# Attention and two MLPs on one core: high parts written in place, rows of maxima in one DMA, longer lags in the plan

## The chip, the cores and the metric

The kernel runs on one core of a Trainium2 chip. The metric is device microseconds of an execution; less is better.

## The reference

Queries are averaged in pairs of neighbours, so that 576 queries meet 1152 keys in each of 16 heads (2 batches of 8, head size 64). The heads are put side by side and go through two MLPs (512 to 2048 to 512), the first with a leaky ReLU, the second with SiLU. All is fp32.

```
q_pool = q.reshape(B, H, S // 2, 2, D).mean(axis=3)
scores = (1 / sqrt(D)) * q_pool @ k^T
attn = exp(scores - max(scores)); attn = attn / (sum(attn) + 1e-9)
x = (attn @ v), heads side by side: 1152 x 512
x = leaky_relu(x @ w_in, 0.01) @ w_out
h = x @ w2_in;  out = (h * sigmoid(h)) @ w2_out
```

## The kernel before

TensorE's fast fp32 form (FP32R) keeps too few bits, so operands are split into a high and a low part, which are multiplied apart and added in PSUM. Two heads j = 0, 1 make a pair p, of which there are eight; head j lies on partitions `own[j]` of what is loaded, the other half is `oth[j]`.

Preparing a pair (`prep`, from pair 1 on). K and Q of both heads are loaded (`knat`, `qnat`; one buffer each), GpSimd adds the two neighbouring queries (L481). ScalarE writes the high parts of both heads to `kf` and `qf` (L348), VectorE the low parts in place (L500, L505; for pair 1 GpSimd). DMAs on SP's queue then bring the parts to where TensorE wants them: `K2[p, j]` holds the high part of K on `own[j]` and the low part on `oth[j]`, `QH[p, j]` the high part of Q on both halves. `copy_ka` copies the high part of K once more to `KA`, whose other half is ones; `QL` holds the low part of Q and, on one row of its other half, minus the maxima of the scores. A score tile (`scores`, L661) is then two matmuls, K2 with QH and KA with QL, and already has the maximum taken off. Pair 0 (`prep_first`) is prepared in smaller pieces without these moves: ScalarE writes the high parts, and the second half of QH is a cast on VectorE for head 0 (L350).

Maxima come first and from high parts of Q alone: `max_tile` multiplies 128 queries by 384 keys (L574, L575, L578; 27 tiles a pair), VectorE reduces each tile to one column of `mx` (L582), `finish_max` reduces these to `mn` (L626), and `finish_rows` sends each column of 128 maxima as a row to QL by a DMA of its own. Pair 0 does it with whole rows of keys in three banks (L602, L607).

After the scores ScalarE takes the exps (L665), TensorE multiplies them with V (`pv`, L693), GpSimd adds them up over the key tiles (L682). `sums` adds over partitions (L721), and since the sums then lie in four rows, they go through DRAM and back (`d`, `cmp`) to be spread over 128 partitions for the reciprocal on VectorE (L756), through DRAM again (`d2`), and are broadcast to all partitions (`r`). `finish` multiplies the product with V by r on VectorE (L796), ScalarE writes its high part `xh` (L799), VectorE the low part `xl` (L800).

Six PSUM banks serve scores, maxima and sums in turn; two hold the product with V. A tile of maxima keeps its bank until VectorE has reduced it.

The order on every engine is made by `Plan`: a list of tasks with weights, lags, due times and tokens for buffers. Time in the plan goes forward, each engine takes the ready task with the earliest due time, and what is emitted then is that engine's order in the program. Due times are given in pairs of length `T` after `T0`: loads at `load`, the preparation at `prep`, maxima between the two values of `max`, the final product at `norm`. A wrong lag in the plan costs nothing by itself, but engines work in order, so that an instruction that is put too early holds what is behind it. The MLPs (L1058 on) have a plan of their own.

Of the kernel before, what the change touches and what calls it, by code (L numbers as in the profile page):

```python
# [18 lines left out]
def pooled_attention_two_mlps(  # L19
# [26 lines left out]
    t0=16.0,  # L46
    t=27.0,
    load=-1.7,
    prep=(-1.4, -1.35, -1.25, -1.15),
    prep1=(10.0, 11.0, 12.0, 13.0),  # L50
    max=(-0.97, -0.2),
    pv=4.0,
    sums=1.15,
    norm=1.55,
    dve_add=(),
    dve_last=tuple((t, j) for t in range(1, 9) for j in range(2)),
    k_pool=((1, 1), (0, 1)),
    lead=3,
    load0=8.0,
# [224 lines left out]
def attention(ctx, tc, q, k, v, xh, xl, weights, end_p):  # L284
# [141 lines left out]
    def prep_first(p, j, loads, out):  # L426
# [46 lines left out]
    def prep(p, loads, due, out):  # L473
# [34 lines left out]
        def move(src, dst, after, d):  # L508
            go = lambda: tuple(y.bitcast(F32) for y in (dst(), src()))
            return dma(d, go, after=after, lag=3.0)  # L510
# [5 lines left out]
        for i in range(n):  # L516
            take = () if i else ("kf",)
            kh.append(add("ACT", 0.21 + 0.84 / n, due[1], k_hi(i), after=[loads["k"][i], x], order=kh[-1:], take=take))
            kl.append(add(eng, 1.95 * w / n, due[1], k_lo(i), after=kh[-1:]))
        qh = add("ACT", 0.63, due[0], q_hi, after=[x])  # L520
        ql = add(eng, w, due[2], q_lo, after=[qh])
        users = {"kf": list(kl), "knat": [], "qnat": []}
        for j in range(2):
            d = due[2] + 0.2 * j
            a = move(lambda j=j: kf[p][own[j]], lambda j=j: K2[p, j][own[j]], kh, d)
# [4 lines left out]
            users["kf"].append(a)  # L530
            users["knat"] += bs
            cs = [move(lambda j=j: qf[p][own[j]], lambda j=j, r=r: QH[p, j][r], [qh], d) for r in own]
# [3 lines left out]
            for i in range(2):  # L536
                out["k", j, i] = [a] + bs
                out["kh", j, i] = [a]
# [7 lines left out]
    def copy_ka(p, j, out, due, after):  # L546
# [5 lines left out]
        else:  # L552
            go = lambda: (KA[p % 2, j][own[j]].bitcast(F32), K2[p, j][own[j]].bitcast(F32))
            out["ka", j, 0] = out["ka", j, 1] = [dma(due, go, after=out["kh", j, 0] + after, lag=3.0)]
# [3 lines left out]
    def max_tile(p, n, out, due):  # L558
# [9 lines left out]
        def pe():  # L568
# [61 lines left out]
    def finish_rows(p, j, units, t, out, due, after):  # L630
        for u in units:
            if u < NFULL:
                rows = [(j, slice(u * 128, (u + 1) * 128), slice(0, 128))]
            else:
                rows = [(i, slice(NFC, SQ), own[i]) for i in range(2)]
            for i, cs, ps in rows:
                go = lambda u=u, i=i, cs=cs, ps=ps: (
                    QL[p % 3, i][orow[i]:orow[i] + 1, cs].bitcast(F32), box["m", p, j][ps, u:u + 1].bitcast(F32)
                )
                out.setdefault(("mr", i), []).append(dma(due, go, after=[t] + after, lag=1.9))  # L640
# [46 lines left out]
    def pv(p, t, due, after, order):  # L687
        def go():
            for c in range(2):
# [8 lines left out]
        last = t == NKT - 1  # L698
        return add("PE", 1.27, due, go, after=after, order=order, take=() if t else ("v",), give=("vnat",) if last else ())
# [14 lines left out]
    def sums(p, after, due):  # L714
# [110 lines left out]
    for p in range(NP):  # L825
# [448 lines left out]
```

## Time and profile before

| | us |
|---|---|
| median of three runs | 681.51 (679.25 to 681.9) |
| profiled execution | 682.97 |
| its span, first to last instruction | 680.9 |
| PE busy | 648.1 |
| VectorE, GpSimd, ScalarE busy | 437.0, 392.3, 302.6 |
| granted TensorE clock, mean | 0.979 |

A busy PE overlaps its matmuls, so its busy time says where it idles and not how full it is. The granted clock is a share of full speed. The profile has three stages: a head until the first scores at 22.8 us, attention until 275.7 us, the MLPs until the end.

### The profile page before, as it was taken

Reading aid. Unit: us, or ns where it says so; the run is one execution under the profiler, and the core shown is the slowest. Engines: PE = TensorE matmul, PEld = TensorE weight load, DVE = VectorE, ACT = ScalarE, POOL = GpSimd, SP = SyncE. Lnnn points to the kernel's source line nnn. Section 1 sums busy time; section 2 is a strip of 40 time slices with the busy share of each in tenths; the row PEclk is TensorE's granted clock in tenths of the full one; section 3 lists DMA queues with packets and bytes.
Section 4 is the critical chain, followed back from the end, with each engine's and each line's share of the span. In section 5 each row is a group of like instructions: output and inputs, shape, how many; then the busy total and the mean of one; then the engine's idle time right before and its main releaser. Section 6 shows DMA issues by size and latency. Waiting matters only on the chain.

```text
span 680.9 us, 9990 instructions
## 1 busy us (share of the span) xinstructions
PE 648.1 (95%) x3616; PEld 523.2 (77%) x3616; DVE 437.0 (64%) x616; ACT 302.6 (44%) x629; POOL 392.3 (58%) x278
## 2 busy tenths in 40 slices
PE   3799999989798999999999999999999999999997
PEld 2566666656565666798998998989998898888986
DVE  7383748639484776686666676688989888522222
ACT  3345545546364555655443343355455553322120
POOL 8578979678696770575354354376666445432120
PEclk9899999979797999999999999999999999999999
DMA  8685556758584711032223223222223322000012
GB/s 208 134 232 158 121 160 139 205 129 240 134 226 93 164 49 50 6 120 92 94 93 94 93 92 94 94 93 84 80 86 123 124 94 93 0 1 1 0 47 93
DMA packets 36248, 72.08 MB, mean 106 GB/s; under 512 B 15820, under 2 KB 15848, under 8 KB 36200
## 3 DMA queue, kind: packets, MB, share of 16 engines
q1 hardware_dynamic: 36200, 71.46, 37.7%
q8 instruction: 28, 0.46, 0.3%
q14 instruction: 20, 0.16, 0.1%
HBM read 49.81 MB, written 2.42 MB: 77 GB/s over the span
## 4 chain that ended last, share of the span: by engine, by line
PE 80%; DMA 9%; DVE 7%; SPq 2%; issue 1%; ACT 1%; POOL 0%; DVEq 0%; POOLq 0%; ACTq 0%
PE ph L1058 30%; PE po L1129 15%; PE pf L1178 14%; PE psum L661 8%; PE psum L693 7%; DMA r<-d 3%; DVE mx L582 3%; PE psum L578 3%; SPq L343 2%; DMA ql<-mn 2%; DMA d<-sum 2%; PE psum L602 1%; DVE pvs L796 1%; DMA qnat<-in_q_dram 1%; DVE mn L607 1%
## 5 line engine op out<-in xcount | busy, mean ns | idle before, releaser
L1111 POOL TENSOR_TENSOR gl<-a,gh 128x512 fp32r<-128x512 f32 (+1 forms) x64 | 97.2, 1519 | 142.7 <-ACT gh L1105 76.1
L682 POOL TENSOR_TENSOR acc<-acc,e 128x576 f32<-128x576 f32 x98 | 147.5, 1533 | 24.0 <-ACT e L665 23.7
L665 ACT ACTIVATE e<-psum 128x288 f32<-128x288 f32 x288 | 102.5, 411 | 97.1 <-PE psum L661 81.7
L582 DVE TENSOR_REDUCE mx<-psum 128x1 f32<-128x384 f32 x189 | 93.9, 547 | 59.4 <-PE psum L578 56.2
L1058 PE MATMUL ph<-xh,w0h 128*128 128x320 f32 (+1 forms) x384 | 109.0, 338 | 0.5 <-ACT pvs L707 0.5
L1058 PE MATMUL ph<-xh,w0l 128*128 128x320 f32 (+1 forms) x384 | 108.7, 337 | 0.0
L1058 PE MATMUL ph<-xl,w0h 128*128 128x320 f32 (+1 forms) x384 | 108.6, 337 | 0.0
L661 PE MATMUL psum<-qh,k 128*128 128x288 f32 x288 | 93.5, 339 | 9.8 <-DVE mx L582 9.1
L661 PE MATMUL psum<-ql,ka 128*128 128x288 f32 x288 | 85.1, 310 | 4.7 <-DMA ql<-mn 3.8
L693 PE MATMUL psum<-e,vnat 128*64 128x288 f32 x576 | 89.3, 434 | 0.0
L661 PEld LDWEIGHTS psum<-qh,k 128*128 128x128 f32 x288 | 57.8, 201 | 38.6 <-DVE mx L582 13.9
L1058 PEld LDWEIGHTS ph<-xh,w0h 128*128 128x128 f32 x384 | 67.7, 188 | 8.2 <-ACT pvs L707 1.0
L132 DVE TENSOR_SCALAR wt<-wt 128x512 f32<-128x512 f32 x56 | 40.3, 720 | 50.3 <-ACT wt L128 50.3
L1058 PEld LDWEIGHTS ph<-xh,w0l 128*128 128x128 f32 x384 | 66.9, 188 | 5.6
L1058 PEld LDWEIGHTS ph<-xl,w0h 128*128 128x128 f32 x384 | 66.9, 188 | 5.0
L167 POOL TENSOR_TENSOR w1l<-wt,w1h 128x512 fp32r<-128x512 f32 x32 | 44.4, 1396 | 40.3 <-ACT w1h L163 40.2
L661 PEld LDWEIGHTS psum<-ql,ka 128*128 128x128 f32 x288 | 58.4, 203 | 5.6 <-DMA ql<-mn 4.4
L167 POOL TENSOR_TENSOR w0l<-wt,w0h 128x512 fp32r<-128x512 f32 x32 | 45.2, 1412 | 24.7 <-ACT w0h L163 24.7
L693 PEld LDWEIGHTS psum<-e,vnat 128*64 128x64 f32 x576 | 36.2, 140 | 29.8 <-issue 16.0
L136 DVE TENSOR_SCALAR wt<-wt 128x512 uint32<-128x512 uint32 x56 | 57.9, 1033 | 1.7
L1178 PE MATMUL pf<-w1h,gl 128*128 128x512 f32 x144 | 56.2, 390 | 0.0
L1178 PE MATMUL pf<-w1l,gh 128*128 128x512 f32 x144 | 56.1, 390 | 0.0
(88 smaller groups left out, 1067.7 us busy)
## 6 DMA issues: line engine op xcount, KB each, us to landing
wraw<-in_moe_w_in_dram SPq DMA_DIRECT2D x32, 512.0 KB, 3.8
wraw<-in_moe_w_out_dram SPq DMA_DIRECT2D x32, 512.0 KB, 9.4
vnat<-in_v_dram SPq DMA_DIRECT2D x8, 576.0 KB, 6.7
k<-kf SPq DMA_DIRECT2D x14, 288.0 KB, 3.6
ka<-k SPq DMA_DIRECT2D x14, 288.0 KB, 6.0
knat<-in_k_dram SPq DMA_DIRECT2D x6, 576.0 KB, 5.9
qnat<-in_q_dram SPq DMA_DIRECT2D x6, 576.0 KB, 6.8
qh<-qnat SPq DMA_DIRECT2D x24, 144.0 KB, 2.7
```

Source lines behind the costliest of these rows:

```text
L132: nc.vector.tensor_scalar(out=tf, in0=tf, scalar1=2.0, scalar2=W_TOP, op0=ALU.max, op1=ALU.min)
L136: nc.vector.tensor_scalar(out=t, in0=t, scalar1=4, scalar2=1, op0=ALU.logical_shift_left, op1=ALU.logical_shift_right)
L167: self.nc.gpsimd.tensor_tensor(out=lo, in0=tf, in1=hi, op=ALU.subtract)
L582: nc.vector.tensor_reduce(out=mx[p][:, n:n + 1], in_=ps[:, 0:KC], op=ALU.max, axis=AX.X)
L661: nc.tensor.matmul(out=ps[:, 0:C], lhsT=lhsT[:, ks], rhs=rhs[:, cs], start=not last, stop=last)
L665: nc.scalar.activation(out=e_t[p, j, t][:, cs], in_=ps[:, 0:C], func=ACTF.Exp, scale=scale)
L682: e.tensor_tensor(out=acc[p, j], in0=e_t[p, j, 0] if t == 1 else acc[p, j], in1=e_t[p, j, t], op=ALU.add)
L693: nc.tensor.matmul(out=vps[p, c][own[j], 0:C], lhsT=vnat[p][:, j, t, :], rhs=e_t[p, j, t][:, c * C:(c + 1) * C], start=(t == 0), stop=(t = ...
L1058: nc.tensor.matmul(out=box[x][:, c, 0:n], lhsT=wt[:, kk, fs], rhs=m[:, kk, chunk(g, c)], start=(kk == 0 and wt is wh and m is xh), stop=(k ...
L1111: nc.gpsimd.tensor_tensor(out=gl, in0=box["a", x], in1=gh, op=ALU.subtract)
L1129: nc.tensor.matmul(out=box[x][:, c, 0:n], lhsT=wt[:, f, ms], rhs=y[:, c * n:(c + 1) * n], start=(f == 0 and wt is oh and y is gh), stop=(f ...
L1178: nc.tensor.matmul(out=box[x][:, 0, :], lhsT=y[:, ts], rhs=wt[:, f, :], start=(f == 0 and y is gh and wt is oh), stop=(f == FB - 1 and y i ...
```

## The change

Five things are changed, all in attention.

- From pair 1 on ScalarE writes the high parts of K and Q straight to K2 and QH on the partitions where they already lie, beside `kf` and `qf`, which stay for the low parts. The DMA from `kf` to K2 and one of two DMAs a head to QH are dropped; the other half of QH is now copied by DMA from the first. For pair 0 the second half of QH is written by ScalarE for head 0 too.
- A tile of maxima from pair 1 on takes every fourth query instead of 128 in a row, so that four columns of `mn` are 512 maxima in order; one DMA writes them. The last 64 queries of a head keep theirs.
- DMAs of the moves, of the chain of sums and of the rows of maxima have longer lags in the plan (`lag` = 4).
- `T0`, `T`, `load`, `prep`, `max` and `norm` have other values.
- `pv` can take several key tiles in one task; `last_pv` gives it one each, as before.

```diff
-    t0=16.0,
-    t=27.0,
-    load=-1.7,
-    prep=(-1.4, -1.35, -1.25, -1.15),
+    t0=22.0,
+    t=26.5,
+    load=-2.0,
+    prep=(-1.6, -1.55, -1.45, -1.4),
-    max=(-0.97, -0.2),
+    max=(-1.1, -0.35),
-    norm=1.55,
+    norm=1.7,
...
-            if j == 0:
-                up = add("DVE", 0.06 + n / 960, d + 0.4 + 0.3 * i, lambda cs=cs: copy("DVE", QH[p, j][oth[j], cs], QH[p, j][own[j], cs]), after=[hi])
-            else:
-                up = add("ACT", 0.22 + n / 1400, d + 0.4 + 0.3 * i, lambda cs=cs: copy("ACT", QH[p, j][oth[j], cs], q2[p][own[j], cs]), after=[x])
+            up = add("ACT", 0.22 + n / 1400, d + 0.4 + 0.3 * i, lambda cs=cs: copy("ACT", QH[p, j][oth[j], cs], q2[p][own[j], cs]), after=[x], order=[hi])
...
+        at_home = {}
+        for j in range(2):
+            go = lambda j=j: copy("ACT", QH[p, j][own[j]], q2[p][own[j]])
+            at_home["q", j] = add("ACT", 0.63, due[0], go, after=[x])
+            at_home["k", j] = []
+            for i in range(n):
+                go = lambda i=i, j=j: copy("ACT", K2[p, j][own[j], cols[i]], keys(i)[own[j]])
+                at_home["k", j].append(add("ACT", 0.21 + 0.84 / n, due[1] + 1.0, go, after=[loads["k"][i], x]))
...
-            a = move(lambda j=j: kf[p][own[j]], lambda j=j: K2[p, j][own[j]], kh, d)
+            a = at_home["k", j]
...
-            cs = [move(lambda j=j: qf[p][own[j]], lambda j=j, r=r: QH[p, j][r], [qh], d) for r in own]
+            cs = [at_home["q", j], move(lambda j=j: QH[p, j][own[j]], lambda j=j: QH[p, j][oth[j]], [at_home["q", j]], d)]
...
-                nc.tensor.matmul(out=ps[:, 0:KC], lhsT=QH[p, j][:, t * 128:(t + 1) * 128], rhs=K2[p, j][:, ks], start=True, stop=True)
+                nc.tensor.matmul(out=ps[:, 0:KC], lhsT=QH[p, j][:, t:NFC:NFULL], rhs=K2[p, j][:, ks], start=True, stop=True)
...
+        full = [u for u in units if u < NFULL]
+        if len(full) > 1:
+            cs = slice(full[0] * 128, (full[-1] + 1) * 128)
+            rows.append((j, cs, lambda: box["m", p, j][:, full[0]:full[-1] + 1], len(full)))
...
-        x = dma(due, down, after=[x])
-        x = dma(due, up, after=[x])
+        x = dma(due, down, after=[x], lag=P["lag"] - 1.0)
+        x = dma(due, up, after=[x], lag=P["lag"])
...
-        x = dma(due, down2, after=[x], lag=3.0)
-        y = dma(due, lambda: up2(0), after=[x], lag=3.0)
-        return [y, dma(due, lambda: up2(1), after=[x], order=[y], lag=3.0)]
+        x = dma(due, down2, after=[x], lag=P["lag"] - 1.0)
+        y = dma(due, lambda: up2(0), after=[x], lag=P["lag"] + 2.0)
+        return [y, dma(due, lambda: up2(1), after=[x], order=[y], lag=P["lag"] + 2.0)]
```

What the plan makes of it shows in three queues. First VectorE before the change, in the middle of pair 3's scores: `cmp` is the reciprocal of pair 2's sums, `pvs` the product of pair 2 with r, `mx` reductions of tiles of maxima of pair 4, `mn` its maxima of head 0 (128x5) and head 1 (128x4), `qnat` and `knat` low parts of pair 5.

```order
L500 TENSOR_TENSOR qnat<-qnat 128x576
L756 RECIPROCAL cmp<-cmp 128x9
L582 TENSOR_REDUCE mx<-psum 128x1 x2
L505 TENSOR_TENSOR knat<-knat,kf 128x1152
L582 TENSOR_REDUCE mx<-psum 128x1 x8
L626 TENSOR_REDUCE mn_1336<-mx 128x5
L582 TENSOR_REDUCE mx<-psum 128x1
L796 TENSOR_TENSOR pvs<-pvs,r 128x576
L582 TENSOR_REDUCE mx<-psum 128x1 x2
L800 TENSOR_TENSOR xl<-pvs,xh 128x576
L582 TENSOR_REDUCE mx<-psum 128x1 x3
L626 TENSOR_REDUCE mn_1398<-mx 128x4
```

The same stretch of VectorE's queue after the change.

```order
L499 TENSOR_TENSOR qnat<-qnat 128x576
L590 TENSOR_REDUCE mx<-psum 128x1 x2
L634 TENSOR_REDUCE mn_1246<-mx 128x5
L590 TENSOR_REDUCE mx<-psum 128x1 x2
L776 RECIPROCAL cmp<-cmp 128x9
L590 TENSOR_REDUCE mx<-psum 128x1 x4
L504 TENSOR_TENSOR knat<-knat,kf 128x1152
L590 TENSOR_REDUCE mx<-psum 128x1 x5
L634 TENSOR_REDUCE mn_1353<-mx 128x4
L816 TENSOR_TENSOR pvs<-pvs,r 128x576
L590 TENSOR_REDUCE mx<-psum 128x1 x3
L820 TENSOR_TENSOR xl<-pvs,xh 128x576
```

The product with r has moved from among pair 4's tiles to behind the last of them, so that only tiles of pair 5 stand behind it.

Next SP's queue in the same place, before: `cmp` and `d` are the way of the sums through DRAM, `r` the broadcasts, `qh`, `k` and `ql` the moves of pair 5.

```order
L343 DMA cmp<-d_1190 128x9
L343 DMA qh_1212<-qnat 64x576 x2
L343 DMA qh_1214<-qnat 64x576
L343 DMA k_1211<-kf 64x1152
L343 DMA d_1261<-cmp 128x9
L343 DMA k_1213<-kf 64x1152
L343 DMA qh_1214<-qnat 64x576
L343 DMA ql_101<-qnat 64x576
L343 DMA ql_106<-qnat 64x576
L343 DMA k_1211<-knat 64x1152
L343 DMA k_1213<-knat 64x1152
L343 DMA r<-d_1261 64x576 x2
```

And SP's queue after, for the sums of pair 1, where the preparation is that of pair 4 and `mn` are maxima of pair 3; it reads alike for the pairs that follow.

```order
L345 DMA cmp<-d_885 128x9
L345 DMA qh_861<-qh_861 64x576
L345 DMA ql_100<-qnat 64x576
L345 DMA ql_105<-qnat 64x576
L345 DMA ql_99<-mn_950 1x128x4
L345 DMA ql_99<-mn_950 1x64x1
L345 DMA ql_104<-mn_950 1x64x1
L345 DMA d_981<-cmp 128x9
L345 DMA r<-d_981 64x576 x2
L345 DMA k_858<-knat 64x1152
L345 DMA k_860<-knat 64x1152
L345 DMA ql_104<-mn_1057 1x128x4
```

The broadcasts of r now stand ahead of the moves of low parts of K, and no move of `kf` is left.

Last ScalarE's queue where pair 6 is prepared, before; `e` are exps of pair 4, `w0h` and `psum` weights of the MLPs.

```order
L728 ACTIVATE sum<-psum,tiny 128x288
L665 ACTIVATE e<-psum 128x288 x2
L163 ACTIVATE w0h<-wt 128x512
L128 ACTIVATE psum<-wraw 128x512
L665 ACTIVATE e<-psum 128x288 x4
L348 ACTIVATE qnat<-qnat 128x576
L348 ACTIVATE kf<-knat 128x1152
L665 ACTIVATE e<-psum 128x288 x14
```

After, where pair 6 is prepared.

```order
L350 ACTIVATE qnat_1370<-qnat_1370 128x576
L350 ACTIVATE qh0_1455<-qnat_1370 64x576
L679 ACTIVATE e_1501<-psum_94 128x288 x2
L350 ACTIVATE qh1_1457<-qnat_1370 64x576
L679 ACTIVATE e_1515<-psum_94 128x288 x2
L350 ACTIVATE kf_1537<-knat_1381 128x1152
L350 ACTIVATE k20_1454<-knat_1381 64x1152
L679 ACTIVATE e_1541<-psum_94 128x288 x2
L679 ACTIVATE e_1550<-psum_94 128x288 x2
L350 ACTIVATE k21_1456<-knat_1381 64x1152
```

Four copies have joined `qf` (written over `qnat`) and `kf`, and exps stand between most of them.

## Rows read from the trace of the kernel before

**Rows 1.** Stages: stretch, length, busy us of PE, PEld, VectorE, ScalarE, GpSimd, granted clock, DMA share, GB/s

```profile
0.00:22.78 22.78, 12.06 (x30) 8.22 (x31) 17.33 (x18) 8.27 (x14) 18.85 (x24) 1.00 0.62 156
22.78:275.73 252.95, 234.62 (x1421) 156.42 (x1419) 158.80 (x286) 132.46 (x343) 180.55 (x122) 0.95 0.60 150
275.73:680.86 405.13, 401.42 (x2168) 358.56 (x2168) 260.89 (x313) 161.84 (x273) 192.90 (x132) 1.00 0.23 75
```

**Rows 2.** The same view by pair: pair 1, pair 7, and the sum of pairs 1 to 7

```profile
58.49:84.94 26.45, 26.11 (x174) 18.21 (x172) 17.87 (x32) 15.35 (x42) 23.41 (x16) 1.00 0.61 156
...
251.48:275.73 24.25, 23.47 (x163) 15.01 (x161) 15.69 (x23) 14.82 (x44) 2.68 (x2) 1.00 0.14 38
sum 217.24, PE 202.34 PEld 134.74 DVE 139.95 ACT 117.22 POOL 156.50; mean PE 28.91 PEld 19.25 DVE 19.99 ACT 16.75 POOL 22.36
```

**Rows 3.** What PE waited for: us in total, times, longest

```profile
PE psum L602 <- DVE qh L350: 10.0, 2, 8.0
PE psum L661 <- DVE mx L582: 9.1, 4, 3.5
PE psum L661 <- DMA ql<-mn: 3.8, 3, 2.2
PE psum L574 <- ACT e L665: 1.5, 1, 1.5
PE psum L578 <- DVE mx L582: 1.1, 2, 0.8
```

**Rows 4.** The tile r: idle time that it ended (us, times), and its DMAs

```profile
  DMA r<-d: 13.7, 3
...
DMA to landing us min/median/max: 2.9/4.7/6.9
```

**Rows 5.** Stretches at half clock between 40 us and the MLPs, columns as in rows 1

```profile
143.98:150.81 6.83, 6.28 (x24) 4.65 (x24) 3.19 (x8) 3.49 (x9) 4.04 (x3) 0.50 0.31 80
178.11:184.94 6.83, 6.62 (x24) 4.63 (x25) 4.47 (x10) 2.76 (x7) 2.34 (x2) 0.50 0.31 77
212.25:219.08 6.83, 6.50 (x23) 4.51 (x24) 4.75 (x11) 2.87 (x7) 2.82 (x2) 0.50 0.04 3
```

**Rows 6.** Timelines of PE and VectorE, 120 to 145 us: start, us, what [idle before]

```profile
120.76 0.69 PE L721 MATMUL psum<-acc,ones 128*32 128x288 f32 x8
...
143.25 0.76 DVE L796 TENSOR_TENSOR pvs<-pvs,r 128x576 f32<-128x576 f32 x1 [4.20 <-DMA r<-d]
...
144.53 0.61 PE L661 MATMUL psum<-qh,k 128*128 128x288 f32 x1 [2.82 <-DVE mx L582]
```

**Rows 7.** DMA issues: line, engine, KB each, median us to landing

```profile
k<-kf SPq DMA_DIRECT2D x14, 288.0 KB, 3.6
...
ql<-mn SPq DMA_DIRECT2D x64, 0.5 KB, 2.4
```

**Rows 8.** The head: timelines of VectorE, SP and PE, 7 to 30 us

```profile
7.11 0.81 DVE L350 CAST qh<-qh 64x256 fp32r<-64x256 f32 x1
...
10.72 1.64 DVE L350 CAST qh<-qh 64x320 fp32r<-64x320 f32 x1
...
26.55 0.73 SPq L343 DMA_DIRECT2D ql<-mn  x1
...
29.86 0.61 PE L661 MATMUL psum<-ql,ka 128*128 128x288 f32 x1 [2.16 <-DMA ql<-mn]
```

**Rows 9.** Timeline of ScalarE at 129 us

```profile
129.09 0.68 ACT L348 ACTIVATE qnat<-qnat 128x576 fp32r<-128x576 f32 x1 [3.28 <-POOL qnat L481]
```

**Rows 10.** Groups by shape: count, busy us, mean ns of one, idle before

```profile
L578 PEld LDWEIGHTS psum<-k,qh 128*128 128x128 f32 x168 | 28.8, 191 | 15.7 <-issue 7.4 <-DVE mx L582 5.2 <-ACT qnat L348 0.9
L348 ACT ACTIVATE kf<-knat 128x1152 fp32r<-128x1152 f32 x6 | 7.0, 1160 | 0.0
L575 PEld LDWEIGHTS psum<-k,qh 128*64 128x64 f32 x21 | 2.8, 135 | 0.0
L348 ACT ACTIVATE k<-knat 64x640 fp32r<-64x640 f32 x2 | 1.5, 726 | 0.0
```

More of the change, by code (lines that the diff above doesn't have):

```diff
@@ L57 @@
     k_pool=((1, 1), (0, 1)),
+    last_pv=tuple((t,) for t in range(9)),
     lead=3,
+    lag=4.0,
     load0=8.0,
@@ L509, in move @@
             go = lambda: tuple(y.bitcast(F32) for y in (dst(), src()))
-            return dma(d, go, after=after, lag=3.0)
+            return dma(d, go, after=after, lag=P["lag"])
         eng, w = ("POOL", 1.45) if halves else ("DVE", 1.0)
@@ L518, in prep @@
             kh.append(add("ACT", 0.21 + 0.84 / n, due[1], k_hi(i), after=[loads["k"][i], x], order=kh[-1:], take=take))
-            kl.append(add(eng, 1.95 * w / n, due[1], k_lo(i), after=kh[-1:]))
         qh = add("ACT", 0.63, due[0], q_hi, after=[x])
-        ql = add(eng, w, due[2], q_lo, after=[qh])
+        at_home = {}
[6 more added lines that the diff above has]
+                at_home["k", j].append(add("ACT", 0.21 + 0.84 / n, due[1] + 1.0, go, after=[loads["k"][i], x]))
+        for i in range(n):
+            kl.append(add(eng, 1.95 * w / n, due[1] + 0.5, k_lo(i), after=[kh[i]], order=[at_home["k", j][i] for j in range(2)]))
+        ql = add(eng, w, due[2], q_lo, after=[qh], order=[at_home["q", j] for j in range(2)])
         users = {"kf": list(kl), "knat": [], "qnat": []}
@@ L529, in prep @@
             ]
-            users["kf"].append(a)
             users["knat"] += bs
-            cs = [move(lambda j=j: qf[p][own[j]], lambda j=j, r=r: QH[p, j][r], [qh], d) for r in own]
+            cs = [at_home["q", j], move(lambda j=j: QH[p, j][own[j]], lambda j=j: QH[p, j][oth[j]], [at_home["q", j]], d)]
             users["qnat"] += cs
@@ L536, in prep @@
             for i in range(2):
-                out["k", j, i] = [a] + bs
-                out["kh", j, i] = [a]
+                out["k", j, i] = a + bs
+                out["kh", j, i] = a
             out["qu", j] = [cs, cs]
@@ L553, in copy_ka @@
             go = lambda: (KA[p % 2, j][own[j]].bitcast(F32), K2[p, j][own[j]].bitcast(F32))
-            out["ka", j, 0] = out["ka", j, 1] = [dma(due, go, after=out["kh", j, 0] + after, lag=3.0)]
+            out["ka", j, 0] = out["ka", j, 1] = [dma(due, go, after=out["kh", j, 0] + after, lag=P["lag"] + 1.0)]
     def max_tile(p, n, out, due):
@@ L630, in finish_rows, with go @@
     def finish_rows(p, j, units, t, out, due, after):
[L631 to L640, printed above, removed]
+        full = [u for u in units if u < NFULL]
+        rows = []
+        if len(full) > 1:
+            cs = slice(full[0] * 128, (full[-1] + 1) * 128)
+            rows.append((j, cs, lambda: box["m", p, j][:, full[0]:full[-1] + 1], len(full)))
+        else:
+            rows += [(j, slice(u * 128, (u + 1) * 128), lambda u=u: box["m", p, j][:, u:u + 1], 1) for u in full]
+        if NFULL in units:
+            rows += [(i, slice(NFC, SQ), lambda i=i: box["m", p, j][own[i], NFULL:NFULL + 1], 1) for i in range(2)]
+        for i, cs, src, n in rows:
+            def go(i=i, cs=cs, src=src, n=n):
+                row = QL[p % 3, i][orow[i]:orow[i] + 1, cs].bitcast(F32)
+                return row, src().bitcast(F32)
+            lag = 2.1 if p == 0 else P["lag"] - 1.0
+            out.setdefault(("mr", i), []).append(dma(due, go, after=[t] + after, lag=lag))
     def scores(p, t, j, out, due, before):
@@ L685, in sum_up, with pv, step @@
         return add("DVE" if on_dve else "POOL", 0.85 if on_dve else 1.45, due, go, after=after, order=order, take=take)
-    def pv(p, t, due, after, order):
+    def pv(p, ts, due, after, order):
         def go():
+            for t in ts:
+                step(t)
+        def step(t):
             for c in range(2):
@@ L696, in go @@
                     )
-        last = t == NKT - 1
-        return add("PE", 1.27, due, go, after=after, order=order, take=() if t else ("v",), give=("vnat",) if last else ())
+        last = ts[-1] == NKT - 1
+        w = 0.25 + 0.98 * len(ts)
+        return add("PE", w, due, go, after=after, order=order, take=() if ts[0] else ("v",), give=("vnat",) if last else ())
     def evac_pv(p, after, due):
@@ L865, in attention @@
         last = []
-        for t in range(NKT):
-            x = pv(p, t, at((2 * t + 1) / (2 * NKT)) + P["pv"], ex[t, 0] + ex[t, 1] + ([] if t else [value]), last)
+        for ts in P["last_pv"] if p == NP - 1 else [(t,) for t in range(NKT)]:
+            after = [x for t in ts for j in range(2) for x in ex[t, j]] + ([] if ts[0] else [value])
+            x = pv(p, ts, at((2 * ts[-1] + 1) / (2 * NKT)) + P["pv"], after, last)
             last = [x]
-            for j in range(2):
-                add("-", 0.0, 0.0, lambda t=t, j=j, p=p: e_t.pop((p, j, t)), after=[x, av[max(t, 1), j]], give=(("e", p, t, j),))
+            for t in ts:
+                for j in range(2):
+                    add("-", 0.0, 0.0, lambda t=t, j=j, p=p: e_t.pop((p, j, t)), after=[x, av[max(t, 1), j]], give=(("e", p, t, j),))
         for j in range(2):
```

## Prediction, made before the changed kernel was run

> **What bounds the kernel now.** I read the stages first, then what TensorE waits for, then its granted clock, then the engine that each long wait points to. The two MLPs take 405.1 of 680.9 us with PE busy for 401.4, at full clock [rows 1]. The change leaves the order of every engine there as it was, so nothing is to be had there. Attention takes 253.0 us after a head of 22.8, and its clock is 0.95 on average. Where nothing disturbs it a pair of heads takes 26.45 us (pair 1); the last, which prepares no other, takes 24.25; pairs 1 to 7 together take 217.24, where seven undisturbed ones would be some 183 [rows 2]. So over 30 us of attention are not PE's own work. Four names lead the list of its waits: the casts of QH on VectorE (10.0 us, in the head), the reductions of maxima on VectorE (9.1), the rows of maxima (3.8) and an exp on ScalarE (1.5) [rows 3].
>
> The 9.1 us are not slow reductions. VectorE works in order, and in its queue stands `pvs * r`, which waits for the DMA that brings r, the reciprocals of an earlier pair's sums. It sat idle 13.7 us for that, in three waits [rows 4]. Meanwhile reductions queued behind it keep their PSUM banks, and PE runs out of banks: 2.82 us at 144.53, and likewise 3.48 and 2.45 us. Each time the granted clock then fell to half, the lower of its two levels, for 6.83 us, in which PE was busy 6.28, 6.62 and 6.50 us [rows 5, 6].
>
> **The change, part by part.** *The three waits for r.* The sums of pair 2 are multiplied at 120.76, and the product with their reciprocals begins at 143.25, as soon as r is there: 22.5 us later [rows 6]. After the change the plan counts the DMAs of this chain as longer, and so puts the product later. Counted in the order of PE, from the sums to the fifth tile of maxima whose reduction stands behind the product (about where banks run out), there were 44 score matmuls, 6 PV steps and 21 tiles; now there are 64, 8 and 22. Of a pair's work (72, 9 and 27) that is about two thirds before and 0.87 now: at the 26.45 us of an undisturbed pair some 18 us before and 23 now, against 22.5 us measured for r. The chain also gets shorter, since SP issues r ahead of the moves of low parts and without two moves of 288 KB in between. So I take all three as gone: 2.82 + 3.48 + 2.45 = 8.75 us of waits, and half of the 19.4 busy us at half clock, 9.7. Sum **18.4**; bounds 6 (one of three goes) and 20 (the same with its small waits).
>
> *Rows of maxima.* Ten DMAs of a pair become four, and maxima are due earlier against the scores. Of 80 such DMAs before, 64 write 128 values of 4 bytes each [rows 7]. Of the 3.8 us of waits for them 2.16 lie in the head, the other **1.6** later [rows 3, 8]; I take them as gone (0 to 1.6). In PE's order the last tile of maxima now stands some 8 us of work ahead of the next pair, before 5.
>
> *Loads earlier.* At 129.09 ScalarE had waited 3.28 us for the pooling of q, with exps queued behind it; PE lost 1.5 us to that [rows 3, 9]. Loads move from 0.3 of a pair ahead of the preparation to 0.4: **1.5** goes (0 to 1.5).
>
> *Small waits.* The other waits for reductions (9.1 + 1.1, less 8.75) come to 1.45 us [rows 3]; with VectorE no longer held I take **1** of them.
>
> *High parts in place.* Pairs 1 to 7 lose the move of kf (14 DMAs of 288 KB [rows 7]) and half of those of QH, but ScalarE still writes kf and qf, because the low parts need them. It gains two copies of 64x1152 and two of 64x576 a pair. 64x640 took 726 ns and 128x1152 1160 [rows 10], so I count 2 x 1.16 + 2 x 0.7 = 3.7 us a pair, 26 in all. ScalarE is busy 117 of the 217 us [rows 2], so the sum is hidden; the burst is what counts. Before, qf and kf stood together (1.8 us) ahead of waiting exps; now kf and one copy do (2.3 us), and the rest stands between exps. One burst of that kind, with a wait ahead of it, cost PE 1.5 us; the list of waits has no second one [rows 3]. I charge 0.25 us a pair, **-1.5** (0 to -9). Fewer bytes I count as nothing: where moves are not waited for they are hidden.
>
> *Tiles of maxima with a stride.* So that one DMA can write a head's 512 maxima in order, a tile now takes every fourth column of QH as weights. What that costs no row shows. Loads of 128 columns take 191 ns and of 64 columns 135 [rows 10], so 128 columns stream in about 110 ns, behind the matmul before them. If the stride doubled that, each of 168 tiles would show 0 to 110 ns more: 0 to 18 us. I take 0, since loads have room: in the seven pairs they are busy 134.7 us beside 202.3 of matmuls [rows 2].
>
> [...]
>
> *The head.* Both casts of QH (0.81 and 1.64 us) leave VectorE for ScalarE, where each follows its high part at once [rows 8]. The first tile then waits only for the low part of K, 0.7 us earlier; the second cast stood between reductions that follow one another, 1.6 us. The last row of maxima was issued at 26.55, behind moves of kf, and PE stood still until 29.86 [rows 8]. ScalarE's new copies of pair 1 (some 3.7 us) fall ahead of the first exps and just fit. I take **3** (1 to 5).
>
> Sum by these terms: 18.4 + 1.6 + 1.5 + 1 + 3 - 1.5 = 24. There is a second way to count: all pairs at the pace of pair 1, with two more tiles (26.8 us): 6 x 26.8 + 24.25 = 185 instead of 217.24 [rows 2], so 32, and 3 for the head, less 1.5: 33.5. The first misses gaps too short for the list of waits; the second allows no new wait. I take **27** between them. The profiled execution took 682.97 us, 1.5 above the median of the three runs, 681.51. So 654.5 against the median; I say **655**.
>
> **The rivals.** *1. The wait for r stays* (0.09): if r needs more than 23 us after the sums, the bank runs out again, each time with the clock behind it: 655 + 18 = 673. For it speaks that two DMAs through DRAM and two broadcasts (median 4.7 us [rows 4]) stay in the chain; against it, that the chain loses its neighbours.
>
> *2. Strided loads cost something* (0.17): 50 to 110 ns on each of 168 tiles, 8 to 18 us: 663 to 673.
>
> [...]
>
> *4. ScalarE's bursts become a wait in each pair* (0.10): 1.5 us in six pairs give 664; if each also halves the clock as the wait for r did (3.2 us more) 683, no change. Against it: five other bursts of before (qf and kf, 1.8 us) have no entry in the list of waits [rows 3].
>
> *5. GpSimd becomes the bound* (0.04): its work of a pair does not shrink, and it is busy 156.5 us in seven pairs, 154 of them in the first six [rows 2], so 25.6 a pair, against 27 of PE. With a tenth more by contention, pairs would take 28: 661.
>
> **How the numbers follow.** My forecast, steady pairs near 27 us, has 0.55, and reaches from 648 to 661. The two rivals on the loads have 0.22, the others 0.23. The range from **647 to 673** leaves out rival 3, the worse half of 4 and some of 1. A difference under 0.5% (3.4 us) can hardly be told from none: faster by more than that **0.88**, within it **0.06**, slower **0.06**.
>
> **What would show it.** Right: no idle time of VectorE before the product for r, or none that PE follows; no stretch at half clock between 40 us and the MLPs; pairs of 26.5 to 28 us; scores from about 21 us; the MLPs from about 249 us, still 405 us long. Strided loads show in the time of a load of maxima, now 191 ns, and in the distance between two tiles. Bursts show as PE waits for exps behind copies. I am wrong if half clock stays once a pair, or if a pair takes over 29 us.

## The result, and the profile after

The changed kernel took 669.96 us (median of 4 runs, 668.94 to 670.55), the kernel before beside it 681.49. The ratio is 0.984 (95% interval 0.981 to 0.986): 11.5 us faster where 26.5 were forecast, and inside the range. The profiled execution of after took 670.55 us, its span 668.7.

The stages of after, split at the first score, the first score of pair 1 and the first matmul of the MLPs; columns as in [rows 1]:

```profile
0.00:20.80 20.80, 11.85 (x31) 8.30 (x31) 15.35 (x16) 10.75 (x19) 16.08 (x22) 1.00 0.68 170
20.80:60.18 39.38, 34.88 (x172) 24.93 (x170) 19.56 (x37) 20.58 (x46) 26.66 (x19) 0.91 0.58 144
60.18:261.85 201.67, 199.32 (x1250) 143.01 (x1249) 146.71 (x249) 133.47 (x325) 155.90 (x107) 1.00 0.48 130
261.85:668.70 406.85, 403.01 (x2168) 359.60 (x2168) 261.25 (x313) 161.91 (x273) 192.85 (x132) 1.00 0.23 75
```

Beside [rows 1, 2] the difference of the spans, 12.2 us, falls apart like this (pair 0 of before is 252.95 less 217.24):

| stretch | before | after | difference | forecast |
|---|---|---|---|---|
| to the first score | 22.78 | 20.80 | -2.0 | |
| pair 0 | 35.71 | 39.38 | +3.7 | head, both together: -3 |
| pairs 1 to 7 | 217.24 | 201.67 | -15.6 | -24 |
| MLPs | 405.13 | 406.85 | +1.7 | 0 |

Attention from pair 1 on runs at full clock, and PE is busy for 199.3 of 201.7 us. Its waits in after (us in total, times, longest) answer [rows 3]:

```profile
PE psum L610 <- ACT qh L350: 7.4, 1, 7.4
PE psum L586 <- DMA k<-e: 2.7, 1, 2.7
PE ph L1080 <- ACT pvs L727: 2.4, 1, 2.4
PE psum L610 <- DVE mn L615: 1.5, 4, 0.5
PE psum L675 <- ACT e L679: 1.4, 1, 1.4
PE psum L586 <- ACT e L679: 0.3, 1, 0.3
```

Between 51 and 259 us there is no wait of PE left, so what the change was charged with there (r, rows of maxima, bursts of ScalarE) is not what is missing. But a PE without waits can still be slow. The tiles of maxima by shape (count, busy us, mean ns of one), beside the first row of [rows 10]:

```profile
L586 PEld LDWEIGHTS psum<-k,qh 128*128 128x128 f32 x168 | 47.4, 318 | 13.7 <-issue 4.5 <-DMA k<-e 2.9 <-DVE mx L590 2.9
L586 PE MATMUL psum<-k,qh 128*128 128x384 f32 x168 | 63.4, 447 | 3.1 <-DMA k<-e 2.7 <-ACT e L679 0.3
```

A load of every fourth column takes 318 ns; side by side it took 191.

The new wait ahead of the MLPs (2.4 us) has 3.41 us of half clock behind it (the second row; the first is in pair 0 and begins late in the wait for `k<-e`):

```profile
34.04:40.86 6.82, 5.94 (x19) 4.16 (x20) 3.71 (x8) 2.63 (x4) 2.77 (x3) 0.50 0.50 169
262.73:266.14 3.41, 3.41 (x10) 2.48 (x8) 1.62 (x2) 1.72 (x4) 3.41 (x3) 0.50 0.00 0
```

The clock of 1.00 in the row of the head is no reading, and part of the 0.91 of pair 0 neither. The trace of after has no record of the clock ahead of 27.21 us (that of before none ahead of 24.51), and a stretch without one is shown as 1.00. Until there scores follow each other every 0.24 us, as they do in the stretch at half clock of before at 30 us, and behind it every 0.13:

```profile
26.91 0.44 PE L675 MATMUL psum<-qh,k 128*128 128x288 f32 x1
27.15 0.33 PE L675 MATMUL psum<-ql,ka 128*128 128x288 f32 x1
...
27.59 0.30 PE L675 MATMUL psum<-qh,k 128*128 128x288 f32 x1
27.72 0.29 PE L675 MATMUL psum<-ql,ka 128*128 128x288 f32 x1
```

So pair 0 of after runs at the lower pace for 6.4 us more than the rows say, pair 0 of before for 1.7.

### The profile page after: what moved, and what is told of

It reads as the page before. It is cut to its first block, busy times and chain, and to the rows that moved or that the text cites. A ratio compares the mean times of both kernels' runs of the same rounds, so it can differ in the third digit from the quotient of the medians.

```text
span 668.7 us, 9922 instructions
## 1 busy us (share of the span) xinstructions
PE 649.1 (97%) x3616; PEld 535.8 (80%) x3616; DVE 442.9 (66%) x614; ACT 326.7 (49%) x661; POOL 391.5 (59%) x278
## 4 chain that ended last, share of the span: by engine, by line
PE 93%; ACT 2%; DMA 2%; POOL 1%; DVE 1%; issue 0%; SPq 0%; ACTq 0%; DVEq 0%
PE ph L1080 30%; PE po L1151 15%; PE pf L1200 15%; PE psum L675 12%; PE psum L712 12%; PE psum L586 7%; DMA k<-e 1%; DMA qnat<-in_q_dram 1%; PE psum L741 1%; PE psum L583 1%; PE psum L582 1%; ACT k L350 1%; POOL k L439 0%; SPq L345 0%; ACT e L679 0%
## 5 line engine op out<-in xcount | busy, mean ns | idle before, releaser
L590 DVE TENSOR_REDUCE mx<-psum 128x1 f32<-128x384 f32 x189 | 96.4, 549 | 61.2 <-PE psum L586 54.9
L675 PE MATMUL psum<-qh,k 128*128 128x288 f32 x288 | 88.6, 324 | 1.4 <-ACT e L679 1.4
L712 PE MATMUL psum<-e,vnat 128*64 128x288 f32 x576 | 86.3, 422 | 0.0
L675 PE MATMUL psum<-ql,ka 128*128 128x288 f32 x288 | 81.5, 299 | 0.0
L675 PEld LDWEIGHTS psum<-qh,k 128*128 128x128 f32 x288 | 56.3, 196 | 27.6 <-issue 14.9
L586 PE MATMUL psum<-k,qh 128*128 128x384 f32 x168 | 63.4, 447 | 3.1 <-DMA k<-e 2.7
L586 PEld LDWEIGHTS psum<-k,qh 128*128 128x128 f32 x168 | 47.4, 318 | 13.7 <-issue 4.5
L712 PEld LDWEIGHTS psum<-e,vnat 128*64 128x64 f32 x576 | 35.4, 137 | 27.2 <-issue 12.4
L1106 ACT ACTIVATE gh<-ph 128x512 fp32r<-128x512 f32 (+1 forms) x32 | 20.9, 652 | 74.2 <-PE ph L1080 74.2
```

The costliest lines, as they stand in the source:

```text
L586: nc.tensor.matmul(out=ps[:, 0:KC], lhsT=QH[p, j][:, t:NFC:NFULL], rhs=K2[p, j][:, ks], start=True, stop=True)
L590: nc.vector.tensor_reduce(out=mx[p][:, n:n + 1], in_=ps[:, 0:KC], op=ALU.max, axis=AX.X)
L675: nc.tensor.matmul(out=ps[:, 0:C], lhsT=lhsT[:, ks], rhs=rhs[:, cs], start=not last, stop=last)
L712: nc.tensor.matmul(out=vps[p, c][own[j], 0:C], lhsT=vnat[p][:, j, t, :], rhs=e_t[p, j, t][:, c * C:(c + 1) * C], start=(t == 0), stop=(t = ...
```

## Experiments

Ratios below are to the kernel before, run beside each kernel, with 95% intervals.

### The stride

**One line undone.** The theory: the strided load is the loss. The rivals: contention with the copies, or another engine that bounds the pairs anyway.

```diff
-lhsT=QH[p, j][:, t:NFC:NFULL]
+lhsT=QH[p, j][:, t * 128:(t + 1) * 128]
```

> Changed kernel with one line undone: the tiles of maxima read their 128 columns of QH side by side again; everything else, one DMA for a head's row of maxima too, stays. The rows of maxima then hold the maxima of other queries, so each softmax is shifted by another query's maximum (the ratio of exponentials to their sum does not depend on the shift). Theory A (the strided weight load is dear: 318 against 191 ns on 168 tiles, and 100 to 127 ns more from one tile to the next): the time falls by 168 x 0.10 to 0.127 = 17 to 21 us, to 649 to 653 us; weight loads of these tiles back at about 190 ns and pairs at 26.5 to 27.2 instead of 29.5 us. Theory B (the loads are slow because ScalarE's in-place copies and the transfers read the same memory): loads stay at 300 ns or more, time 667 to 671 us. Theory C (loads get fast, but another engine then sets the pairs): loads at 190 ns, pairs at 28.5 us or more with waits of PE in them, time 660 us or more.

660.54 us, ratio 0.968 (0.966 to 0.971): 9.4 us less than the changed kernel, half of what theory A gave. By the time it could be theory C, but no other engine sets the pairs: PE's longest wait in them is 0.4 us. The loads are back at 196 ns:

```profile
L586 PEld LDWEIGHTS psum<-k,qh 128*128 128x128 f32 x168 | 29.4, 196 | 14.3 <-DVE mx L590 3.9 <-issue 3.1 <-DMA k<-e 3.0
```

Pair 0 and pairs 1 to 7 of this run:

```profile
20.92:59.51 38.59, 34.06 (x172) 23.13 (x171) 20.70 (x37) 20.61 (x46) 24.61 (x19) 0.91 0.54 134
59.51:252.83 193.32, 189.91 (x1251) 129.24 (x1249) 145.84 (x249) 132.98 (x325) 158.80 (x107) 1.00 0.52 138
```

Pairs 1 to 7 take 8.35 us less than in after, with the same matmuls. How a tile shows the load: in both kernels there is a place where a tile, the sums, a tile and a score follow each other (start us, us). First after, then this run:

```profile
123.23 0.44 PE L586 MATMUL psum<-k,qh 128*128 128x384 f32 x1
123.59 0.69 PE L741 MATMUL psum<-acc,ones 128*32 128x288 f32 x8
124.22 0.57 PE L586 MATMUL psum<-k,qh 128*128 128x384 f32 x1
124.62 0.29 PE L675 MATMUL psum<-qh,k 128*128 128x288 f32 x1
```

```profile
119.82 0.34 PE L586 MATMUL psum<-k,qh 128*128 128x384 f32 x1
120.09 0.69 PE L741 MATMUL psum<-acc,ones 128*32 128x288 f32 x8
120.72 0.45 PE L586 MATMUL psum<-k,qh 128*128 128x384 f32 x1
121.00 0.29 PE L675 MATMUL psum<-qh,k 128*128 128x288 f32 x1
```

From a tile to what follows it takes 0.36 and 0.40 us against 0.27 and 0.28, some 0.1 us more, and nothing of that is idle time in the trace. The median from tile to tile is 276 ns against 176, from tile to score 237 against 177. Of some 0.1 us on 168 tiles 9.4 us arrived, 56 ns a tile: about a third of the tiles are followed by a score, where the difference is 60 ns, and some of the gain came back as short waits, 1.1 us of idle time after 60 us that after had not. My 17 to 21 us took the extreme for the mean.

**The stride put into the kernel before.**

```diff
-lhsT=QH[p, j][:, t * 128:(t + 1) * 128]
+lhsT=QH[p, j][:, t:NFC:NFULL]
-rows = [(j, slice(u * 128, (u + 1) * 128), slice(0, 128))]
+rows = [(j, slice(u * 128, (u + 1) * 128) if p == 0 else slice(u, NFC, NFULL), slice(0, 128))]
```

> Kernel before with the stride alone: its tiles of maxima read every fourth column of QH, and the DMA of each column of maxima writes every fourth element of its row; order and everything else unchanged. Theory A (strided load costs by itself): loads of these tiles 310 to 325 ns instead of 191, and PE's busy pairs longer by 24 x 0.10 to 0.127 = 2.4 to 3 us; the three waits for r (8.75 us) and their half clock (9.7 us) may shrink as the pairs grow, so the time rises by 8 to 21 us, to 690 to 702 us. Theory B (in-place copies make the loads slow): loads stay at 190 ns, time 680 to 684 us.

683.61 us, ratio 1.003 (1.001 to 1.005): only 1.9 us more. That the load itself costs is confirmed, without any copy in place:

```profile
L578 PEld LDWEIGHTS psum<-k,qh 128*128 128x128 f32 x168 | 46.6, 318 | 12.9 <-issue 7.4 <-DVE mx L582 1.7 <-ACT e L665 1.0
```

But here the slower tiles fill time in which PE would have waited: the waits in PE's list together fall from 28.2 to 23.9 us, and the three stretches at half clock are 3.41 us each instead of 6.83. So the same edit costs 1.9 us in a kernel that waits and 9.4 in one that doesn't.

**A stride of two columns.**

```diff
-lhsT=QH[p, j][:, t:NFC:NFULL]
+lhsT=QH[p, j][:, t // 2 * 256 + t % 2:t // 2 * 256 + 256:2]
-    rows.append((j, cs, lambda: box["m", p, j][:, full[0]:full[-1] + 1], len(full)))
+    for h in range(0, len(full), 2):
+        cs = slice(h * 128, (h + 2) * 128)
+        rows.append((j, cs, lambda h=h: box["m", p, j][:, h:h + 2], 2))
```

> Changed kernel with a stride of two columns (8 bytes) in place of four (16 bytes) in the tiles of maxima, and two DMAs of [128, 2] for a head's row. [...] If any stride costs the same: loads near 318 ns, 669 to 671 us. If only the full 16-byte stride costs: loads near 190 ns, 650 to 654 us.

665.67 us (0.973 to 0.980 of before). The time fits neither guess (it lies between the two), the loads fit the second:

```profile
L586 PEld LDWEIGHTS psum<-k,qh 128*128 128x128 f32 x168 | 29.6, 200 | 14.2 <-DVE mx L590 4.0 <-issue 3.6 <-ACT e L680 2.4
```

With the stride of 8 bytes a load took 200 ns (192 at least), side by side 196 (186 at least, in the run with one line undone), with the stride of 16 bytes 318 (307 at least). Why the two strides differ so, no run shows. With the 5 us above the run with one line undone go a wait of 2.8 us for an exp at 70 us and 6.83 us of half clock behind it, which that run has not; they are followed up under the last heading.

**Four DMAs a head again, contiguous columns.**

```diff
-lhsT=QH[p, j][:, t:NFC:NFULL]
+lhsT=QH[p, j][:, t * 128:(t + 1) * 128]
...
+go = lambda u=u, i=i, cs=cs, ps=ps: (QL[p % 3, i][orow[i]:orow[i] + 1, cs].bitcast(F32), box["m", p, j][ps, u:u + 1].bitcast(F32))
```

> Changed kernel with contiguous weight columns for the tiles of maxima and, as in the kernel before, one DMA for each column of maxima (four a head and one each for the half tiles): the stride and the one DMA a head are undone together, and the rows of maxima hold the right queries. Theory A (the stride is the whole loss, and the number of DMAs of maxima costs nothing): as the run with one line undone, 649 to 654 us. Rival (the single DMA was worth the 1.6 us that the prediction gave it): 1.5 to 2.5 us above that run, with waits of a score matmul for the row of maxima in every pair.

666.21 us (0.975 to 0.981 of before). Neither theory: 5.7 us above the run with one line undone, and no score waits for a row of maxima. The new waits are others:

```profile
PE psum L586 <- ACT e L673: 2.0, 3, 0.9
PE psum L586 <- DMA k<-knat: 1.9, 1, 1.9
...
PE psum L735 <- POOL acc L690: 1.1, 2, 0.7
```

I take it that the rows of maxima cost by their place on SP, whose queue the loads and moves share (the issues of four take 3.21 us there at 199.73); no run tests that by itself. By the times the single DMA was worth some 5.7 us in this plan, and its stride cost 9.4.

### The waits for r: plan or copies?

**The plan alone**: due times and lags of after in the kernel before.

```diff
-    t0=16.0, t=27.0, load=-1.7, prep=(-1.4, -1.35, -1.25, -1.15), max=(-0.97, -0.2), norm=1.55,
+    t0=22.0, t=26.5, load=-2.0, prep=(-1.6, -1.55, -1.45, -1.4), max=(-1.1, -0.35), norm=1.7, lag=4.0,
-            return dma(d, go, after=after, lag=3.0)
+            return dma(d, go, after=after, lag=P["lag"])
```

> Kernel before with the plan's numbers of the change alone: its due times and the longer counted lags of the DMAs, without the copies in place, the two casts on ScalarE, the single DMA a head or the stride. Theory A (the three waits for r go by the plan's order alone): no wait of a reduction of maxima behind the product with r, no half clock between 50 us and the MLPs, and 8.75 us of waits and some 8.5 us of half clock gone: 664 to 668 us. Theory B (the chain for r must also lose the moves of high parts from its queue, as the changed kernel does): one to three waits of 1 us or more for r stay, each with half clock behind it: 670 to 679 us.

680.69 us, ratio 0.998 (0.996 to 1.001): no gain clear of the noise. The waits of PE behind the product are gone as theory A has it, but the gain that it gave for them did not come. Instead ScalarE is late with exps (waits of PE):

```profile
PE psum L662 <- ACT e L666: 5.4, 3, 3.0
PE psum L575 <- ACT e L666: 5.4, 2, 4.0
PE psum L662 <- ACT sum L729: 3.0, 2, 1.7
```

The largest, followed back: PE waits at 77.36 us for an exp, ScalarE's exps stand behind the high part of Q, that waits for GpSimd's pooling, and the pooling for the load of Q, which SP issued only at 63.89, behind ten rows of maxima (the view begins at 58 us and shows eight), and on which the pooling then waited until 73.84 (timelines of PE, ScalarE, GpSimd and SP):

```profile
77.36 0.69 PE L575 MATMUL psum<-k,qh 128*128 128x384 f32 x1 [3.96 <-ACT e L666]
```

```profile
75.27 0.68 ACT L349 ACTIVATE qnat<-qnat 128x576 fp32r<-128x576 f32 x1 [5.88 <-POOL qnat L482]
```

```profile
73.84 1.40 POOL L482 TENSOR_TENSOR qnat<-qnat 128x576 f32<-128x576 f32 x1 [8.92 <-DMA qnat<-in_q_dram]
```

```profile
57.63 5.59 SPq L344 DMA_DIRECT2D ql<-mn  x8
63.26 0.59 SPq L344 DMA_DIRECT2D knat<-in_k_dram  x1
63.89 0.43 SPq L344 DMA_DIRECT2D qnat<-in_q_dram  x1
```

**The copies alone**: the run with contiguous columns and four DMAs, with the numbers of the plan of before.

```diff
-    t0=22.0, t=26.5, load=-2.0, prep=(-1.6, -1.55, -1.45, -1.4), max=(-1.1, -0.35), norm=1.7, lag=4.0,
+    t0=16.0, t=27.0, load=-1.7, prep=(-1.4, -1.35, -1.25, -1.15), max=(-0.97, -0.2), norm=1.55, lag=3.0,
```

> The run with contiguous columns and four DMAs (666.2 us), with the due times and counted lags of the kernel before: the copies in place and the casts on ScalarE without the new plan. The run with the plan alone had 680.7 us, where waits for exps had taken the place of the waits for r. Theory A (the two parts need each other: the product with r still stands where it stood): one to three waits of 1.5 us or more of score matmuls for reductions behind the product with r, each with half clock: 672 to 680 us. Theory B (r comes early enough once the moves of high parts are gone from SP's queue, the copies in place are what counts): no such wait, 663 to 668 us.

672.94 us (0.981 to 0.990 of before), theory A by the time, at its lower end, but B by the trace: no score waits over 0.7 us for a reduction, VectorE sat idle 1.1 us for r instead of 13.7, and a DMA of r lands in 3.2 us (median) instead of 4.7 [rows 4]:

```profile
  DMA r<-d: 1.1, 1
...
DMA to landing us min/median/max: 2.9/3.2/3.6
```

So the copies alone bring 8.9 us, the plan alone 1.1 (within the noise), both together 15.5 (the run with four DMAs). What is left to the copies alone are smaller waits, 6.9 us for exps, 3.2 for rows of maxima, 5.1 for reductions. With the plan alone VectorE still sat idle 5.1 us for r, in one wait, though the DMAs of r landed in 3.0 us there. So I take the moves that are gone from SP's queue for what brings r early enough; whether their place in the queue counts or their bytes, no run separates.

### Head and end

**A second buffer for the last pair's PV sums.**

```diff
-pvs[p] = end_p.tile([128, 2, C], F32, tag="pvs", name="pvs")
+pvs[p] = end_p.tile([128, 2, C], F32, tag="pvs7" if p == NP - 1 else "pvs", name="pvs")
-take=() if c else ("pvs",)
+take=() if c or p == NP - 1 else ("pvs",)
```

> Changed kernel with a second buffer for the evacuated PV sums of the last pair, so that ScalarE's evacuation no longer stands behind the product, the high and the low part of pair 6; on ScalarE one instruction trades places with two, every other order is the same. Theory A (the wait of 2.35 us ahead of the MLPs and the half clock behind it, 3.41 us, come from that one buffer): 2.35 + 1.7 = 4 us gone, 665 to 667 us, no wait of the first matmul of the MLPs over 0.6 us. Rival (the MLPs then wait for the last high part of x instead): the wait only changes its name, 668.5 to 671 us.

666.90 us (0.977 to 0.980 of before), 3.1 us less than the changed kernel; the wait is 0.5 us, and no half clock follows. This is the chain in after that made the wait, from VectorE and ScalarE:

```profile
258.73 0.75 DVE L816 TENSOR_TENSOR pvs<-pvs,r 128x576 f32<-128x576 f32 x1
260.23 0.76 DVE L820 TENSOR_TENSOR xl<-pvs,xh 128x576 fp32r<-128x576 f32 x1 [0.75 <-ACT xh L819]
```

```profile
259.52 0.68 ACT L819 ACTIVATE xh<-pvs 128x576 fp32r<-128x576 f32 x1 [1.55 <-DVE pvs L816]
261.09 0.71 ACT L727 ACTIVATE pvs<-psum 128x288 f32<-128x288 f32 x2 [0.89 <-DVE xl L820]
```

The product of pair 6 now stands behind VectorE's last additions, the evacuation of pair 7 needs its buffer, and the MLPs need the evacuation's banks.

**Pair 1's high parts of K by DMA, as before.**

```diff
             a = at_home["k", j]
+            if halves:
+                a = [move(lambda j=j: kf[p][own[j]], lambda j=j: K2[p, j][own[j]], kh, d)]
```

> Changed kernel in which pair 1's high parts of K go by DMA from kf as in the kernel before; its Q and the later pairs stay in place. Theory A (the 1.41 us that PE waits for an exp at 23.5 us, and the 2.68 us for the low part of K at 34.9 us with the half clock behind it, come from the four copies of K ahead of them on ScalarE): both waits shrink to under 0.5 us, the half clock of 6.83 us goes or starts elsewhere, 3 to 7 us gone: 663 to 667 us. Rival (moves of 288 KB late on SP's queue take their place): a wait for k<-kf or k<-e of 2 us or more at 30 to 40 us, 668 to 672 us.

672.53 us (0.986 to 0.989 of before), 2.6 us more than the changed kernel. Theory A was right on the waits it names: for the exp 0.2 us stayed of 1.4, for `k<-e` nothing of 2.7. The rival's waits did not come either, and the time lies just above its range. Other waits stand there: 1.3 us for a row of maxima, which on SP now follows a move of `kf`, and 1.9 for exps behind copies of pair 2. The rows give 13.7 us at half clock until 46.3 us instead of 6.8, but that is no difference: the changed kernel runs 6.4 us of pair 0 at the same lower pace without a record. What makes the 2.6 us stays open.

**A way to all of it.** With a stride of two columns, the second buffer and then two changes of loads:

```diff
-    load=-2.0,
+    load=-2.2,
...
-due = 0.0 if p == 0 else P["load1"] if p == 1 else at(P["load"])
+due = 0.0 if p == 0 else P["load1"] if p == 1 else at(P["load"] + 0.35 * (p == 2))
```

> The run with a stride of two columns (665.7 us), with both mends: the second buffer for the last pair and pair 1's high parts of K by DMA. If the mends add up: 665.7 less 4 less 3 to 7, so 655 to 659 us. If the new plan brings waits for exps or for operands as the stride-two run had at 70 us (2.85 us, with 6.83 us of half clock behind it): 660 to 664 us. Not better than the stride-two run: 664 to 668 us.

The stride of two, the second buffer and the moves of pair 1 gave 661.05 us (0.969 to 0.972): the second guess, with a wait of 3.3 us for an exp at 43 us.

> The run with a stride of two columns (665.7 us) and the second buffer for the last pair alone. Theory A (its wait ahead of the MLPs, 2.36 us, and 3.41 us of half clock there, are all that goes): 661 to 662.5 us; the wait for an exp at about 70 us, 2.8 us with half clock behind it, stays. If that wait is chance and comes and goes with the order: none is possible, since every order but two instructions on ScalarE is the same.

Without those moves 663.36 (0.970 to 0.976), above both ends of what I gave. The wait ahead of the MLPs is gone, but the one at 70 us grew from 2.8 us under the same order, so that it is not fixed by the order:

```profile
PE psum L582 <- ACT e L680: 5.1, 1, 5.1
```

> As the run with a stride of two columns and the second buffer, with the loads of a pair due 0.2 of a pair earlier, so that on SP the load of K of pair 3 stands ahead of the rows of maxima of pair 1 that it stood behind. Theory A (the wait for an exp at 70 us comes from those loads: ScalarE waits for GpSimd's pooling, which waits for the load of Q): the wait of 2.8 us and the half clock behind it go, 656 to 659 us. Rival (the earlier load moves other issues late): another wait of 1 us or more takes its place, 660 to 664 us.

With the earlier load, 660.44 (0.966 to 0.973). The wait is 0.8 us, as theory A has it, but not for its reason: SP issued the load of Q that the pooling waits for at 61.16 us, later than at 57.96 in the run before. What got shorter is the time from this issue to the pooling, 6.9 us against 11.5; why stays open. The rival is right on the time, since waits for `k<-e` rose to 3.4 us: the load of pair 2 had moved ahead of the low parts of pair 1.

> The run before (stride of two columns, second buffer, earlier loads; 660.4 us) with one more change: the loads of pair 2 due 0.35 of a pair later, so that on SP they stand behind the four moves of the low parts of K of pair 1 and the copies to KA, not ahead of them. Theory A (the waits of tiles of pair 1 for the low part of K, 1.19 and 2.22 us at 34 to 37 us, come from the loads of 576 KB ahead of those moves): both together fall under 1 us, the half clock at 36 us (6.83 us) goes or shrinks, 655 to 658.5 us. Rival (the low parts are late by GpSimd, which starts them at 22.5 us behind ScalarE's copies): waits of 2 to 3 us stay, 659 to 662 us. A later load may also bring a wait of pair 2's tiles, 1 us or more at 45 to 60 us: 660 to 664 us.

654.36 us, ratio 0.961 (0.957 to 0.964): the fastest here, 15.6 us under the changed kernel, and somewhat more than theory A gave. That it is near the forecast of 655 confirms nothing, since the second buffer and the order of loads are not in the change. On SP the four moves of low parts come first now, and PE's list of waits after the first scores has nothing over 1.4 us:

```profile
25.89 3.21 SPq L345 DMA_DIRECT2D k<-e  x4
29.15 0.58 SPq L345 DMA_DIRECT2D knat<-in_k_dram  x1
```

```profile
...
PE psum L676 <- ACT e L680: 1.4, 1, 1.4
PE ph L1081 <- ACT pvs L728: 0.5, 1, 0.5
```

No stretch at half clock is on record ahead of the MLPs, where the run before had two of 6.83 us, at 22.5 and 36.2 us. Only the second is a gain: the record begins at 26.85 us here, and scores are 0.24 us apart until there, while the run before had gone at full pace from 19.1 to 22.5 us. From the first score to the MLPs it takes 226.8 us instead of the changed kernel's 241.1:

```profile
20.80:247.59 226.79, 223.48 (x1420) 150.81 (x1419) 164.71 (x284) 152.99 (x370) 183.69 (x124) 1.00 0.53 140
```

## Why the prediction was wrong, step by step

The forecast was 27 us, the profiled executions differ by 12.2. The three parts of the table make up the 15 us that are missing.

**The step that failed: tiles of maxima with a stride, taken as 0.** They cost 9.4 us, 8.35 of it in pairs 1 to 7. The bounds, 0 to 18 us, held it, and the second rival names it, 8 to 18 us with a chance of 0.17; the choice of the end was wrong. For rival 3, the other 0.05 of the 0.22 on the loads, no run shows a cause: a load took 127 ns more, and the kernel stayed 11.5 us faster than before. I chose 0 because loads were busy for 134.7 us beside 202.3 of matmuls. A sum over seven pairs says nothing on the room of one load: from tile to tile there were 176 ns with loads of 196, and 276 with loads of 318. The estimate that doubling adds 110 ns to a load was near: 318 less 191 is 127. Where a row of the same shape was missing, the size that the bound itself gave should have been taken, with the distances between tiles as the cover.

**The head, 3 us forecast, 1.7 lost.** The first scores came 2.0 us earlier, as worked out. But "fall ahead of the first exps and just fit" failed: the copies of pair 1 fill ScalarE until 23 us, PE waited 1.41 us for an exp behind them, and GpSimd started the low parts of K only at 22.49. PE then waited 2.7 us for these:

```profile
20.47 2.52 ACT L350 ACTIVATE k<-e 64x576 fp32r<-64x576 f32 x4
```

```profile
23.48 0.61 PE L675 MATMUL psum<-qh,k 128*128 128x288 f32 x1 [1.41 <-ACT e L679]
...
34.92 2.31 PE L586 MATMUL psum<-k,qh 128*128 128x384 f32 x6 [2.68 <-DMA k<-e]
```

These waits are only some 1 us more than the 0.94 and 2.16 us that pair 0 of before spent on others, and in both kernels 6.83 us at half clock go with the longer one. Of the rest of the 3.7 us, 0.8 went with the stride (38.59 us in the run with one line undone), and some 1.6 are an estimate for the lower pace until 27.2 us: half of 5.0 us of work against half of 1.7. Why that pace lasts longer than before stays open. I had looked at what each cast frees and not at who waits for the copies. The last run shows how much of the waits is the order of loads on SP: with the same copies the second one is gone.

**The end, not seen.** 1.7 us in the MLPs is half clock behind the wait of 2.4 us. That wait replaces the 0.5 us of before, since the plan puts the product of pair 6 behind VectorE's last additions too, and pair 6 has only the last pair, with its one buffer, to hide in. It comes with the plan: 2.4 us with the plan alone, 0.5 with the copies and the old plan. Which of the plan's numbers does it, no run shows. I had written that nothing changes in the MLPs.

**What held.** Pairs 1 to 7 without the stride take 193.32 us, 23.9 less than before: the 24 us that 27 less the head leaves. That it fits so closely is luck, since 27 was chosen between two counts 9.5 us apart, and 2.4 us of the 193.32 are the wait ahead of the MLPs that I had not seen. The three waits for r and their half clock are gone. The reason that I gave for it, the plan, holds only together with the copies, which I had charged 1.5 us and which alone brought 8.9. A wait of PE for ScalarE's bursts did not come after 51 us (0.3 us at 50); a copy of 64x1152 took 1.16 us, as priced. GpSimd did not bound: from pair 1 to the MLPs it was busy for 155.9 us of 201.67. Of the second way of counting (33.5 us) the pace was wrong: pair 1 of before has 174 matmuls [rows 2], where the steady pair of the run with one line undone has 184 in 27.84 us, against 29.50 in after:

```profile
119.20:148.70 29.50, 29.50 (x184) 21.42 (x182) 19.75 (x35) 19.80 (x46) 25.40 (x18) 1.00 0.48 124
```

```profile
115.94:143.78 27.84, 27.84 (x184) 19.11 (x182) 20.43 (x35) 19.79 (x46) 25.74 (x18) 1.00 0.50 132
```

I had added two tiles for that and left out a step of PV. So for the pairs the first count, 21 us without the head, was too low, the second, 30.5, too high, and the value between them came out.

## What to carry to other kernels

Set the time of one load of weights beside the distance from tile to tile (here 196 ns beside 176, with the stride 318 beside 276), and don't ask whether there is room on average; where columns were interleaved here, a load took 200 ns with a stride of two fp32 values and 318 with one of four. The slower loads cost little while the engine waited anyway (1.9 us here), and far more once those waits were gone (9.4), so price a side effect in the kernel that the change makes. When an operand comes late on a queue that works in order, look at what else stands in it: with fewer moves VectorE's wait for r fell from 13.7 to 1.1 us, with other due times alone to 5.1. And where a view shows a full clock from the start, compare it with the distance of matmuls (here 0.24 us where no clock was on record, 0.13 at full clock).

## What I had not expected of the hardware

A load of 128 columns of 128 fp32 values took 186 ns at least side by side and 307 with a stride of 16 bytes, both with copies in place on ScalarE and without, and 192 with a stride of 8 bytes. The profile showed nothing of it as idle time: it was in the duration of loads (318 ns against 196) and in the distance of tiles (276 against 176). At half clock the stride showed next to nothing: the eleven tiles in the stretch at 34 us loaded in 329 ns (mean) with the stride of 16 bytes and in 323 side by side, in the run with one line undone. And half clock was not tied to a place: the kernel before had it at 143.98, 178.11 and 212.25 us [rows 5], and in the last run, whose longest wait of PE after the first score is 1.4 us, none is on record from 26.85 us to the MLPs.
